# A list scheduler's view of its transfers: places in a queue instead of one rate, and a new table of shifts

## The chip, the core and the metric

The kernel runs on one core of one Trainium2 chip. A core has five engines with a queue of instructions each: PE (matrix products), ACT (activation functions), DVE (vector work), POOL (a second, slower vector engine) and SP, which here only issues transfers (DMAs). The engines run side by side and wait for each other by semaphores. The metric is the device time of one execution in microseconds (us); three runs of the kernel before gave 899.85, 899.12 and 898.61, so the median is 899.12 us.

## The reference

One transformer block on x, 2048 tokens of 1024 numbers in bfloat16. The attention is computed in four segments of 512 tokens, with 32 heads of width 32, and carries a memory M from segment to segment:

```python
x1 = layernorm(x)
q, k, v = (split_heads(x1 @ w) for w in (wq, wk, wv))       # each 1024 x 1024
for s in range(4):                                          # segments of 512 tokens
    a_dot = softmax(q[s] @ k[s].T * scale + mask) @ v[s]
    a_mem = (phi(q[s]) @ M) / (phi(q[s]) @ z + 1e-6)        # phi(t): t + 1 if t > 0, else exp(t)
    o[s] = g * a_mem + (1 - g) * a_dot                      # g = sigmoid(beta), one per head
    M += phi(k[s]).T @ v[s];  z += phi(k[s]).sum(rows)
h = x + o @ wo
h2 = h + (silu(layernorm(h) @ w1) * (layernorm(h) @ w3)) @ w2   # w1, w3: 1024 x 3584, w2: 3584 x 1024
```

## The kernel before, in words

The program does not write its instructions in the order in which they run. Each method of the class `Kernel` records operations in a graph (`Graph.op`, L282), with the buffers that they read and write, an estimated cost for each engine that could do them, and a class (a small number goes first). At the end `Graph.schedule` (L341) runs through a model of the five engines in time: whenever an engine is free in the model, it takes the ready operation with the lowest class and, within a class, the lowest number. The order so found on each engine is then emitted (`Graph.emit`, L523), with semaphore waits where an operation depends on another engine or on a transfer. So the costs in the model never reach the chip; the order that they lead to does. In the chip each engine, SP too, follows its order strictly.

Operations are gathered in units, counted up by `stage()`. The table `SHIFT` at the top gives for a unit a number that is added to its operations' numbers and one of -1, 0, 1 that is added to their class. The table is a result of a search and carries no other meaning.

The work, in the order in which `run` records it:

- **q, k, v** (`qkv`, `project`): for each segment and each half of the heads, three weights of 1 MB (1024 x 512) are loaded into one of three buffers `wp` (two later on), and four blocks of 128 x 512 per weight are made by eight matmuls each. In the trace these are L760 with `wp` beside `xnT` or `hnT`, the normalised and transposed x. ACT or DVE copies each block out of PSUM (L783, L784). A `wp` buffer can be loaded anew only when the last matmul that reads it is done.
- **normalisation** (`ln1`): x is loaded into one of four buffers `xs`, normalised by DVE (statistics L887, L890, scaling L902) and transposed by a transfer (`dma_t`, L332) into `xnT`, or into buffers named `hnT` that are free at that time.
- **attention** (`attention`, `scores`, `finish`): for each segment and half, ten groups of score matmuls (L1096) that use PE in four row strips, each followed by an exponential on ACT (L1110, 128 x 2048 numbers) and a mask on POOL (L1119); then column-strip matmuls for sums and products with v (L1197) and for the memory (L1178). The keys' phi is transposed by a transfer too (`pkn<-pk`).
- **normalising factors** (L1243 and on): for segments 2 and 3 the reciprocals are written to DRAM (`r_scr<-T`) and read back with every row repeated over 32 partitions: eight transfers of 256 KB for each half (L1288), four into `R0w` and four into `R`. The retrieval from the memory (L1323, PE in 16 tiles) waits for the four in `R`.
- **output projection** (`wo_stage`): eight matmuls per 128 x 512 block with `wo` and `oT`, x added (L1369), the sum h stored in `h_scr`, normalised and transposed into `hnT`.
- **up and down projection** (`ffn_up`, `ffn_down`): weights `w1b`, `w3b` of 512 KB in two buffers each, seven `w2b` of 1 MB, loaded once; matmuls L760 with `hnT` or `hm`. They fill PE between the pieces of attention of the last two segments, and alone from about 390 us on.

How the old scheduler sees a transfer: SP is busy for 400 ns (a transposition 1250 ns) for the issue; then all transfers are served one after the other at 260 bytes per ns, with the bytes of some kinds scaled by a factor; and the data are there 1560 ns after the service ends:

```python
begin = max(o.end, dma_free)
dma_free = begin + o.bytes / self.DMA_RATE
done = dma_free + self.DMA_FIX
```

All transfers are issued by SP, from `dma` (L325), `dma_t` (L332) or `copies` (L1288). The functions that the diff touches:

## Time and profile before

| | before |
|---|---|
| median of three runs | 899.12 us |
| the profiled execution, its own time | 899.22 us |
| its span, first to last instruction | 897.5 us |
| PE busy | 872.9 us (97%), 5733 recorded matmuls |
| DVE, ACT, POOL busy | 440.6, 303.5, 186.5 us |
| granted PE clock | 1.0 of full speed |
| moved by DMA | 105.75 MB |

The profile is of one execution. "Busy" is time in which the engine works on at least one instruction; matmuls overlap, so their durations do not add up to it. The view of waits puts each idle stretch of an engine down to what ended it: another engine's instruction, a transfer (named by what it writes and reads), or "issue", when nothing that the profile shows was waited for. In SP's timeline an entry is the issue of a transfer, not the transfer itself; from issue to landing is told apart. Some matmuls, 88 of 5821, have no record.

### The profile page before, as it was taken

The numbers are of one execution on the slowest core, as the hardware profiler recorded it, in microseconds if no ns is written. First come the engines' busy times: TensorE is split into PE (matmuls) and PEld (weight loads), VectorE is DVE, ScalarE is ACT, GpSimd is POOL, SyncE is SP. The second block draws the span as 40 slices with busy tenths as digits, with TensorE's granted clock in tenths as the row PEclk, the third lists the DMA queues.
The fourth block names the chain that finished last, engine by engine and source line by source line (L and its number), as shares of the span: only waits on it lengthen the run. The fifth ranks groups of instructions, "written<-read, shape, count | busy, mean of one in ns | idle before, by whom it ended". The sixth has DMA issues, their size and how long they took to land.

```text
span 897.5 us, 13708 instructions
## 1 busy us (share of the span) xinstructions
PE 872.9 (97%) x5733; PEld 398.7 (44%) x5821; DVE 440.6 (49%) x690; ACT 303.5 (34%) x347; POOL 186.5 (21%) x233
## 2 busy tenths in 40 slices
PE   8989899999999999999999999999999999999998
PEld 5343444444434344444444444444444444444445
DVE  5777768777566676747562132113333343323111
ACT  6857685767746464611110010001111111101000
POOL 2544344644352542612100000000000000000000
PEclk9999999999999999999999999999999999999999
DMA  7699867364791728368943014112212232200310
GB/s 238 161 236 228 194 179 175 118 147 125 195 198 56 166 70 165 94 223 228 271 127 95 20 49 116 47 47 76 65 53 74 67 95 61 80 18 1 94 36 24
DMA packets 148796, 105.75 MB, mean 118 GB/s; under 512 B 46336, under 2 KB 134400, under 8 KB 147712
## 3 DMA queue, kind: packets, MB, share of 16 engines
q1 hardware_dynamic: 148736, 104.89, 44.6%
q8 instruction: 46, 0.75, 0.4%
q14 instruction: 14, 0.11, 0.0%
HBM read 84.94 MB, written 9.44 MB: 105 GB/s over the span
## 4 chain that ended last, share of the span: by engine, by line
PE 88%; DMA 7%; DVE 1%; issue 1%; SPq 1%; ACT 1%; POOL 0%; DVEq 0%; ACTq 0%
PE ps L760 82%; PE ps L1197 3%; DMA R<-r_scr 3%; PE ps L1096 2%; DMA wp<-in_A_wq_dram 1%; DMA wp<-in_A_wv_dram 1%; SPq L1288 1%; DMA wp<-in_A_wk_dram 1%; DMA hnT<-xs 1%; DMA r_scr<-T 1%; ACT et L1110 0%; SPq L332 0%; PE ps L1178 0%; DVE oT L1303 0%; PE ps L1323 0%
## 5 line engine op out<-in xcount | busy, mean ns | idle before, releaser
L760 PE MATMUL ps<-hnT,w1b 128*128 128x512 bf16 x876 | 225.1, 379 | 2.0 <-issue 1.3
L760 PE MATMUL ps<-hnT,w3b 128*128 128x512 bf16 x878 | 225.3, 379 | 1.1 <-issue 0.2
L1399 ACT ACTIVATE sg<-ps 128x512 bf16<-128x512 f32 x112 | 66.9, 597 | 413.0 <-PE ps L760 407.9
L760 PE MATMUL ps<-w2b,hm 128*128 128x512 bf16 (+2 forms) x930 | 197.6, 366 | 1.2
L1402 DVE SCALAR_TENSOR_TENSOR t<-sg,ps 128x512 bf16<-128x512 bf16 x112 | 76.8, 686 | 180.1 <-ACT sg L1399 179.8
L1110 ACT ACTIVATE et<-ps 128x2048 bf16<-128x2048 f32 x80 | 150.0, 1875 | 42.6 <-PE ps L1096 42.3
L760 PEld LDWEIGHTS ps<-w2b,hm 128*128 128x128 bf16 x952 | 90.9, 98 | 102.9
L760 PEld LDWEIGHTS ps<-hnT,w3b 128*128 128x128 bf16 x896 | 86.7, 98 | 105.5 <-issue 2.6
L760 PEld LDWEIGHTS ps<-hnT,w1b 128*128 128x128 bf16 x896 | 86.0, 98 | 105.5 <-issue 3.8
L1119 POOL TENSOR_SCALAR_AFFINE_SELECT et<-et 128x512 bf16<-128x512 bf16 x96 | 92.8, 973 | 130.7 <-ACT et L1110 129.2
L1407 DVE SCALAR_TENSOR_TENSOR hm<-t,ps 128x512 bf16<-128x512 bf16 x112 | 76.2, 686 | 62.3 <-PE ps L760 60.9
L1432 DVE TENSOR_TENSOR ob<-hr,ps 128x512 bf16<-128x512 bf16 (+2 forms) x34 | 22.3, 656 | 109.0 <-PE ps L760 108.5
L760 PE MATMUL ps<-hnT,wp 128*128 128x512 bf16 x249 | 60.1, 380 | 4.9 <-DMA wp<-in_A_wk_dram 2.0
L760 PE MATMUL ps<-xnT,wp 128*128 128x512 bf16 (+1 forms) x343 | 60.4, 320 | 3.8 <-DMA wp<-in_A_wk_dram 1.4
L760 PE MATMUL ps<-wo,oT 128*128 128x512 bf16 x252 | 60.0, 379 | 0.2
L1133 DVE TENSOR_TENSOR sum<-sum,et 128x512 bf16<-128x512 bf16 (+1 forms) x64 | 42.8, 673 | 10.4 <-POOL et L1119 5.9
L760 PEld LDWEIGHTS ps<-xnT,wp 128*128 128x128 bf16 x352 | 27.7, 98 | 29.8 <-issue 3.2
L760 PEld LDWEIGHTS ps<-hnT,wp 128*128 128x128 bf16 x256 | 23.1, 98 | 34.1 <-issue 4.1
L760 PEld LDWEIGHTS ps<-wo,oT 128*128 128x128 bf16 x256 | 24.2, 98 | 30.2 <-issue 2.1
L760 PE MATMUL ps<-wp,xnT 128*128 128x512 bf16 x124 | 30.6, 380 | 2.2 <-DMA wp<-in_A_wv_dram 1.8
L1339 POOL TENSOR_TENSOR oT<-Nsb,R 128x512 bf16<-128x512 f32 x22 | 30.0, 1381 | 8.3 <-DVE lnmv L890 5.7
L1096 PE MATMUL ps<-qT,kT 32*128 32x128 bf16 (+3 forms) x512 | 31.7, 301 | 0.0
(97 smaller groups left out, 563.9 us busy)
## 6 DMA issues: line engine op xcount, KB each, us to landing
w1b<-in_B_w_dram SPq DMA_DIRECT2D x28, 512.0 KB, 3.9
w3b<-in_B_w_dram SPq DMA_DIRECT2D x28, 512.0 KB, 4.2
wp<-in_A_wv_dram SPq DMA_DIRECT2D x8, 1024.0 KB, 6.4
wp<-in_A_wk_dram SPq DMA_DIRECT2D x7, 1024.0 KB, 6.5
wp<-in_A_wq_dram SPq DMA_DIRECT2D x7, 1024.0 KB, 5.7
w2b<-in_B_w_dram SPq DMA_DIRECT2D x7, 1024.0 KB, 8.2
xs<-in_A_x_dram SPq DMA_DIRECT2D x16, 256.0 KB, 5.8
h<-in_A_x_dram SPq DMA_DIRECT2D x16, 256.0 KB, 3.4
```

The lines of the kernel that those rows point to most:

```text
L760: return [e.matmul(p[0](gr), p[1], p[2], start=p[3], stop=p[4]) for p in part]
L1096: ins.append(e.matmul(self.bank(gr, j, 512 - 128 * kc, off), k[r, g0 + g, 128 * kc:128 * kc + 128], q[r, g0 + g, 128 * kc:512], start=True ...
L1110: return [e.activation(et[:, :, :], src, AF.Exp, scale=self.scale)]
L1119: self.pool_op(lambda e, v=v, pat=pat: e.affine_select(v, v, pattern=pat, compare_op=ALU.is_ge, fill=0.0, base=0, channel_multiplier=-1), ...
L1133: lambda e, gr: [e.tensor_tensor(out, x, y, op=ALU.add)], reads=[x, y],
L1197: ins.append(e.matmul(self.ps[32 * i:32 * i + 32, b * 512 + c0:b * 512 + c0 + n], lhsT(i, kc, j), rhs(i, j), start=kc == 0 and j == first, ...
L1288: o.emit = lambda e, gr, to=to, src=src: [e.dma_start(to, src)]
L1339: self.either(lambda e, out=out, Ns=Ns, R1=R1: e.tensor_tensor(out, Ns, R1, op=ALU.add), 512, 2, [Ns, R1], [out], 2)
L1399: self.g.op("act", act_ns(512), lambda e, gr, sg=sg: [e.activation(sg, self.bank(gr), AF.Tanh, scale=0.5)], writes=[sg], cls=0, group=gg)
L1402: e.scalar_tensor_tensor(t1, sg, 1.0, self.bank(gr), op0=ALU.add, op1=ALU.mult)], reads=[sg], writes=[t1], cls=0,
L1407: e.scalar_tensor_tensor(dst, t1, 0.5, self.bank(gr), op0=ALU.mult, op1=ALU.mult)], reads=[t1], writes=[dst], cls=0,
L1432: self.g.op("dve", dve_ns(n), lambda e, gr, hs=hs, ob=ob, n=n: [e.tensor_tensor(ob, hs, self.bank(gr, 0, n), op=ALU.add)], reads=[hs], wri ...
```

## The change

Two things change, both in the scheduler's model.

First, a transfer is described by five numbers of its kind in place of its bytes: the time of its issue on SP, the places that it needs in a queue to be issued, the places that it holds while it is served, its time of service, and the time from the end of service to landing. The queue has 128 places. The new method `room` looks at the transfers still being served, lets each give back its places evenly over its service, and says when enough are free; the issue begins then, and SP stands until it ends. The table `LOADS` holds the numbers for twelve kinds; a transposition (`turn`) needs 92 places, a weight (`w`) 20. The nine first loads have a time of service of their own in place of a scale. `copies` and `dma_t` go through the same function `load`.

Second, the table `SHIFT` is another one: 577 entries instead of 570; of the 556 units that both have, five keep their pair. It was chosen by a search over the new model, with copies of the model that were disturbed.

The computation, the buffers, the sizes of the transfers and the numbers of matmuls (5821) and transfers (272) stay the same; the order on every engine is another one, and three operations that either DVE or POOL may do fall to DVE.

```diff
--- before.py
+++ after.py
@@ -28,103 +28,104 @@
 SHIFT = {
-    0: (-224, 0), 3: (7, 1), 4: (125, 0), 5: (120, 0), 6: (30, 0), 7: (0, 1), 8: (-28, 1),
...
-    596: (-75, 0), 597: (246, 0), 598: (3396, -1), 599: (0, 1), 600: (-6, 1),
+    0: (0, -1), 3: (952, 1), 4: (-2010, 1), 5: (170, -1), 6: (3510, 0), 7: (3489, -1),
...
+    597: (0, 1), 598: (224, 1), 599: (-1370, -1), 600: (2374, 1),
 }
...
@@ -193,8 +194,18 @@
     PAGE = 1024
     LAT = {"pe": 260.0, "act": 110.0, "dve": 110.0, "pool": 130.0, "dma": 150.0}
     SWITCH = 105.0
-    DMA_RATE = 260.0
-    DMA_FIX = 1560.0
+    PLACES = 128
+    LOADS = {
+        "x": (438, 56, 6, 717, 1449), "w": (382, 20, 42, 3722, 1419),
+        "first": (436, 30, 68, 1765, 1450), "beta": (339, 20, 12, 86, 2063),
+        "turn": (1240, 92, 38, 923, 1415), "wo": (314, 70, 0, 1236, 1437),
+        "store": (339, 50, 8, 679, 1397), "up": (370, 50, 50, 1872, 1611),
+        "rows": (422, 2, 6, 1208, 1631), "down": (385, 58, 28, 3150, 1386),
+        "hr": (433, 2, 32, 818, 1538), "out": (333, 0, 12, 367, 1011),
+    }
+    KINDS = (("xs", "x"), ("h_scr", "store"), ("r_scr", "store"), ("hr", "hr"), ("hn", "x"),
+             ("h", "x"), ("wp", "w"), ("wo", "wo"), ("w1b", "up"), ("w3b", "up"),
+             ("w2b", "down"), ("beta", "beta"), ("out", "out"))
     BEGIN = 800.0
 
     def __init__(self, nc, es):
@@ -316,22 +327,37 @@
         self.ops.append(o)
         return o
 
-    def dma(self, out, in_, cls=5, deps=(), scale=1.0):
-        n = 1
-        for s in out.shape:
-            n *= s
-        o = self.op("sp", 400.0, None, reads=(in_,), writes=(out,), cls=cls, deps=deps,
+    def load(self, out, in_, emit, kind, cls, deps=(), serve=None):
+        issue, need, held, time, land = self.LOADS[kind]
+        o = self.op("sp", issue, emit, reads=(in_,), writes=(out,), cls=cls, deps=deps,
                     kind="dma")
-        o.emit = lambda e, g: [e.dma_start(out, in_)]
-        o.bytes = n * SIZE[out.dtype] * scale
+        o.load = need, held, serve or time, land
         return o
 
+    def dma(self, out, in_, cls=5, deps=(), serve=None, kind=None):
+        name = out.tensor.name
+        kind = kind or next(k for n, k in self.KINDS if name.startswith(n))
+        return self.load(out, in_, lambda e, g: [e.dma_start(out, in_)], kind, cls, deps, serve)
+
     def dma_t(self, out, in_, cls=5):
 
-        o = self.op("sp", 1250.0, None, reads=(in_,), writes=(out,), cls=cls, kind="dma")
-        o.emit = lambda e, g: [e.dma_start_transpose(out, in_)]
-        o.bytes = 130000
-        return o
+        return self.load(out, in_, lambda e, g: [e.dma_start_transpose(out, in_)], "turn", cls)
+
+    @staticmethod
+    def room(line, now, need):
+
+        line[:] = [x for x in line if x[1] > now]
+        left = [(max(b, now), e, held * (e - max(b, now)) / (e - b)) for b, e, held in line]
+        over = sum(x[2] for x in left) + need - Graph.PLACES
+        t = now
+        for b, e, held in left:
+            if over <= 0:
+                break
+            if held > 0:
+                part = min(over, held)
+                t = b + part / held * (e - b)
+                over -= part
+        return t
 
     def stage(self):
 
@@ -354,6 +380,7 @@
         order = {e: [] for e in ENGINES}
         mode = None
         dma_free = 0.0
+        line = []
         n_done = 0
         seqno = 0
         waiting = []
@@ -452,6 +479,8 @@
                         begin = max(begin, held["dve"])
                     elif e == "dve" and o.port:
                         begin = max(begin, until["pool"])
+                    if o.kind == "dma":
+                        begin = self.room(line, now, o.load[0])
                     o.end = begin + cost
                     until[e] = o.end
                     if e == "dve" and o.port:
@@ -465,8 +494,9 @@
                     done = o.end + lat
                     if o.kind == "dma":
                         begin = max(o.end, dma_free)
-                        dma_free = begin + o.bytes / self.DMA_RATE
-                        done = dma_free + self.DMA_FIX
+                        dma_free = begin + o.load[2]
+                        done = dma_free + o.load[3]
+                        line.append((begin, dma_free, o.load[1]))
                     seqno += 1
                     heapq.heappush(events, (done, seqno, "done", o))
                     if o.users and e == "pe":
@@ -931,7 +961,7 @@
         for i in range(4):
             t = 4 * s + i
             x = self.xs[i][:, :]
-            self.g.dma(x, self.x2d[t * 128:(t + 1) * 128, :], cls=2, scale=0.65)
+            self.g.dma(x, self.x2d[t * 128:(t + 1) * 128, :], cls=2)
             self.ln(t, x, x, 4 + s)
             self.g.dma_t(self.xnT[s][:, :, i * 128:(i + 1) * 128], x, 3)
 
@@ -968,7 +998,7 @@
                 continue
             for kind in "qkv":
                 w, src = self.weights(kind, half)
-                self.g.dma(w[:, :, :], src, cls=1, scale=0.87)
+                self.g.dma(w[:, :, :], src, cls=1)
                 for i in range(4):
                     self.project(s, kind, half, i, w)
 
@@ -978,13 +1008,13 @@
         (wq, sq), (wk, sk), (wv, sv) = (self.weights(kind, 0) for kind in "qkv")
         dma = self.g.dma
         x = [(self.xs[t][:, :], self.x2d[t * 128:(t + 1) * 128, :]) for t in range(4)]
-        loads = [x[0] + (0.66,), x[1] + (0.66,), x[2] + (1.2,),
-                 (wq[:, :, 0:256], sq[:, :, 0:256], 1.19), x[3] + (0.7,),
-                 (wk[:, :, 0:256], sk[:, :, 0:256], 0.89),
-                 (wq[:, :, 256:512], sq[:, :, 256:512], 0.89),
-                 (wk[:, :, 256:512], sk[:, :, 256:512], 0.89), (wv[:, :, :], sv, 1.11)]
-        for out, in_, scale in loads:
-            dma(out, in_, cls=0, scale=scale)
+        loads = [x[0] + (780,), x[1] + (670,), x[2] + (1230,),
+                 (wq[:, :, 0:256], sq[:, :, 0:256], 2400), x[3] + (720,),
+                 (wk[:, :, 0:256], sk[:, :, 0:256], 1790),
+                 (wq[:, :, 256:512], sq[:, :, 256:512], 1790),
+                 (wk[:, :, 256:512], sk[:, :, 256:512], 1790), (wv[:, :, :], sv, 4520)]
+        for out, in_, serve in loads:
+            dma(out, in_, cls=0, serve=serve, kind="x" if serve < 1500 else "first")
         self.applied = []
         for t in range(4):
             self.first_tile(t)
@@ -1271,7 +1301,7 @@
             rm = Rc[:, 1, :, :].rearrange("p j b -> p b j") if not both else Rc[:, :, :, :].rearrange("p t j b -> p b t j")
             G.op("pool", 300.0 + 100 * both, lambda e, gr: [e.tensor_copy(td, rm)], reads=[rm], writes=[td], cls=2)
             self.dve_op(lambda e: e.transpose(T2, T1), dve_ns(512), [T1], [T2], 2)
-            G.dma(rd, T2, cls=2, scale=0.5)
+            G.dma(rd, T2, cls=2)
 
         rd = self.rd[128 * (2 * (s % 2) + half):128 * (2 * (s % 2) + half) + 128, :]
 
@@ -1282,11 +1312,9 @@
             for i in range(4):
                 to = tile[32 * i:32 * i + 32, :, :].rearrange("p j n -> p (j n)")
                 of = rd[32 * i + row:32 * i + row + 4, :]
-                o = G.op("sp", 420.0, None, reads=(of,), writes=(to,), cls=2, kind="dma")
-                o.bytes = 312000
                 src = bass.AP(of.tensor, of.offset, [[0, 32], [1, 2048]])
-                o.emit = lambda e, gr, to=to, src=src: [e.dma_start(to, src)]
-                ops.append(o)
+                ops.append(G.load(to, of, lambda e, gr, to=to, src=src: [e.dma_start(to, src)],
+                                  "rows", 2))
             return ops
 
         rows0 = rows and s in ROWS0
@@ -1356,7 +1384,7 @@
             t = 4 * s + i
             h, hn = self.h[t % 2], self.hn[0]
             self.g.stage()
-            self.g.dma(h[:, :], self.x2d[t * 128:(t + 1) * 128, :], cls=2, scale=0.72,
+            self.g.dma(h[:, :], self.x2d[t * 128:(t + 1) * 128, :], cls=2,
                        deps=(self.mark,) if t < 2 else ())
             for half in range(2):
                 self.g.stage()
@@ -1369,7 +1397,7 @@
                 self.g.op("dve", dve_ns(512), lambda e, gr, hs=hs: [e.tensor_tensor(
                     hs, hs, self.bank(gr), op=ALU.add)], reads=[hs], writes=[hs], cls=1,
                     group=gr)
-            self.g.dma(self.hd[t * 128:(t + 1) * 128, :], h[:, :], cls=3, scale=0.5)
+            self.g.dma(self.hd[t * 128:(t + 1) * 128, :], h[:, :], cls=3)
             self.ln(16 + t, h[:, :], hn[:, :], 6)
             self.g.dma_t(self.hnT[s][:, :, i * 128:(i + 1) * 128], hn[:, :], 2)
 
@@ -1412,7 +1440,7 @@
         if blk == 0:
             for i in range(7):
                 self.g.dma(self.w2[i][:, :, :], self.B_w2[i * 512:(i + 1) * 512, :].rearrange(
-                    "(j p) n -> p j n", p=128), cls=5, scale=0.87)
+                    "(j p) n -> p j n", p=128), cls=5)
         for i in range(8):
             t = 8 * blk + i
             hr = self.hr[t % 3]
```

## The prediction

> **What bounds the kernel now.** I read the page first: its own span line, the busy shares and the chain that ended last.
>
> ```profile
> span 897.5 us, 13708 instructions
> PE 872.9 (97%) x5733; PEld 398.7 (44%) x5821; DVE 440.6 (49%) x690; ACT 303.5 (34%) x347; POOL 186.5 (21%) x233
> PE 88%; DMA 7%; DVE 1%; issue 1%; SPq 1%; ACT 1%; POOL 0%; DVEq 0%; ACTq 0%
> ```
>
> PE is the bound: 897.5 - 872.9 leaves 24.6 us in which it does nothing. Busy PE time cannot be shortened by an order: the clock is 1.0 throughout, and both programs hold the same 5821 matmuls with the same 189 changes between full-array, row-tiled and column-tiled groups (counted in the two orders). So only those 24.6 us are in play. Windows of 50 us tell where they lie (start and end, length, then busy us and count of PE, weight loads, DVE, ACT and POOL, the clock, DMA share and GB/s); this one stands for the nine from 400 us on:
>
> ```profile
> 500.00:550.00 50.00, 49.74 (x229) 22.67 (x232) 12.97 (x19) 4.78 (x8) 0.00 (x0) 1.00 0.19 53
> ```
>
> Its 0.26 us missing are lost records (229 of 232). Behind 400 us nothing is to be had but the last 2.4 us, where the final output leaves. Before 20 us the start waits for x and the first weights (some 3.5 us); both orders issue the same first nine loads. That leaves 20 to 320 us. There the view of waits, for PE alone, says who ended the idle time (us in total, times, longest):
>
> ```profile
> PE ps L760 <- DMA wp<-in_A_wk_dram: 3.4, 2, 2.0
> PE ps L760 <- issue: 2.9, 18, 0.2
> PE ps L760 <- DMA wp<-in_A_wv_dram: 2.7, 3, 1.0
> PE ps L760 <- DMA hnT<-xs: 1.5, 1, 1.5
> PE ps L1197 <- issue: 1.4, 1, 1.4
> PE ps L1323 <- DMA R<-r_scr: 1.2, 2, 0.9
> PE ps L760 <- DMA wp<-in_A_wq_dram: 0.3, 1, 0.3
> ```
>
> Transfers: 3.4 + 2.7 + 1.5 + 1.2 + 0.3 = 9.1 us in nine waits. The 2.9 us of "issue" are sixteen-odd pieces of 0.2 us behind a change of tiling; they stay. The largest wait, in SP's timeline and PE's (start, us, instruction):
>
> ```profile
> 94.46 0.40 SPq L325 DMA_DIRECT2D wp<-in_A_wv_dram  x1
> 95.54 1.92 SPq L332 DMA_TRANSPOSE xnT<-xs  x1
> ...
> 99.38 2.69 SPq L332 DMA_TRANSPOSE hnT<-xs  x1
> 102.17 2.48 SPq L332 DMA_TRANSPOSE pkn<-pk  x1
> 104.70 0.58 SPq L325 DMA_DIRECT2D wp<-in_A_wk_dram  x1
> ```
> ```profile
> 108.25 1.03 PE L760 MATMUL ps<-wo,oT 128*128 128x512 bf16 x4
> 111.27 1.04 PE L760 MATMUL ps<-hnT,wp 128*128 128x512 bf16 x4 [1.99 <-DMA wp<-in_A_wk_dram]
> ```
>
> An issue of L332 takes 1.24 us when little is in flight, and 1.9 to 2.7 here, behind 1 MB of wv. SP issues in order, so the load of wk starts at 104.70 and lands at 111.2, and PE stands for 2 us. Three such places (wk at 111 and 249 us, wv at 241) cost 2.0 + 1.4 + 1.0 = 4.4 us of the 9.1. The old scheduler gave an issue a fixed 1250 or 400 ns and never saw this.
>
> [...] between 94 and 113 us the landings follow the issues, 0.6 to 1.3 us apart for 256 KB. [...] here the up-projection puts 50 into 10.79 us (49 recorded), 215.8 ns.
>
> **The change, part by part.** The capacity of 128 places, the table of costs and `room` exist only in the scheduler; they emit no instruction and no wait. What reaches the chip is another order, chosen through another table of shifts. Counts: PE 5821 and SP 272 in both, DVE 690 to 693, ACT 331 in both, POOL 235 to 232 (three operations that may run on either). Three DVE operations at 0.7 us add 2 us to an engine that is 49% busy; cover: its own idle time; without cover at most 2 us. Cost taken: 0.
>
> The value lies in the distances. For each load I count the PE work from the last matmul that reads the old buffer to the first that needs the new one: 215.8 ns per 512-column matmul, 0.42 us per group of scores (0.65 for some with 256 columns), 0.46 us for the retrieval's sixteen tiled matmuls, 4 to 5 us for a whole column block. Against it stands the need: 5.4 us from issue to landing when alone (median 6.6 over all, with company 6.8), 0.1 us of semaphore and about 0.3 us until the last matmul is through: 5.85 us alone, some 6.9 in company.
>
> ```profile
> DMA to landing us min/median/max: 5.1/6.6/9.3
> ```
>
> Place by place, what before waits for and what the new order does there:
> - wk at 111 (2.0) and wv at 101 (0.9): the crowd on SP is still there (h, wo, three transposes), but wv is no longer ahead of it. Without the 3.7 us of service of 1 MB ahead, the transposes are through before the release. The wq behind them has 24 matmuls, two scores of 0.42 and one of 0.65: 6.67 us. Wk follows with 32 matmuls and four scores: 8.7. I leave 0.5 us at wq.
> - wv at 241 (1.0) and wk at 249 (1.4): now 40 matmuls and four scores (10.1 us) and 24 matmuls with a column block (9.5): both gone.
> - wv at 51 (0.8), wq at 36 (0.3): these two kinds recur: loads with 24 matmuls and two or three scores, 6.0 us against 5.85. Of such places the new order has five (wk three times, wq, wv), most with nothing beside them. I leave 0.2 us each for one with wo behind it and for one of 24 matmuls and the retrieval, 5.18 + 0.46 = 5.64.
> - hnT at 63 (1.5): the transpose is now issued some 33 us of PE work ahead instead of 9: gone.
> - R at 259 and 310 (0.3 and 0.9): distance 24.4 and 15.3 us instead of 16.5 and 14.4. The second also no longer waits for the eighth R row in line: R1 and R0w alternate and PE needs the seventh, 1.2 us less. I leave 0.3.
>
> Left over: 0.5 + 0.4 + 0.3 = 1.2 us. For what distances cannot show (a transposition or store whose DVE input comes late, with weights behind it on SP) I add as much again, 1.3 us: bounds 0 and, if every one of some ten tight loads takes 0.5 us, 5 us. The "issue" wait of 1.4 us in the middle of a column group I don't understand and leave as it is. A stall taken away moves the whole rest forward, since PE is then never idle. Sum: 9.1 - 1.2 - 1.3 = 6.6 us. Profiled execution: 897.5 us of span and 1.7 around it are 899.2; minus 6.6 gives 892.6; the median of 899.12 stands 0.1 under it: **892.5 us**.
>
> What is late next: PE would wait on PSUM evacuations by DVE and ACT. I compared the shortest chain (matmul, evacuation, next matmul in that bank) with the PE work between, for the 298 and 296 such waits up to 400 us: under 0.5 us to spare are 5 before and 9 after, nearly all in the first 10 us, where 0.2 to 0.4 us may be added.
>
> **Rivals.**
> - *Half is given back.* The loads stay tight by design (6.0 against 5.85 us), and one landing of 0.5 to 1 us more in company comes back at six or seven places: 4 us on top of 2.5. Gain 9.1 - 6.5 = 2.6: 896.5 us. For it: wv at 44 us, with a transpose right behind, took 6.8 us instead of 5.4.
> - *Nothing moves.* The transfers were only the last to arrive, and something else (ACT's exponentials, 1875 ns each, or the POOL mask) is ready just behind: 899 +- 1.8. Against it: where PE waited for a transfer the others had been done; for it: DVE is 68 to 80% busy in every 50 us up to 250 us.
> - *Slower, by late evacuations.* The new classes put normalisation (DVE L887, L902) or sums (L1133) in front of evacuations. Each time PE waits one DVE operation, 0.65 us. It turns the sign above 6.6 us, that is from ten such hits, and shows as slower from thirteen; with twenty: 892.5 + 13 = 905.5 us. For it: nearly 300 waits of this kind; against it: before shows one only (0.6 us at 71 us), with much the same spare times.
> - *The change does not do what it says*, the order being nearly the old one: excluded, since PE, DVE and SP orders differ in most places up to 460 us.
>
> **How the numbers follow.** Forecast (887.5 to 895): 0.66. Half given back (895 to 897.3): 0.16. Nothing moves (897.3 to 900.9, 0.2%, about what a measurement of this kernel can tell from no change): 0.08. Slower: 0.10. Faster is 0.66 + 0.16 = 0.82. Range: the low end if all 9.1 go and the odd 1.4 with them: 888.5; the high end takes in the half and some of no change: 898.0.
>
> **What would show it.** Right: in 20 to 320 us PE's waits on wk, wv, hnT and R sum to 1 to 4 us; at the wq load that follows h, wo and three transposes near 100 us SP issues within 0.5 us of the release; PE busy stays 872 to 874 us. Wrong: new waits on wp above 1 us each, PE waits on DVE or ACT above 2 us in sum, or SP lines where a transpose waits for DVE with a weight load behind it.

## The result, and the profile after

| | before | after |
|---|---|---|
| median of 12 runs | 899.49 us (897.39 to 905.36) | 902.23 us (897.20 to 905.05) |
| ratio after / before | | 1.0023, 95% interval 1.0000 to 1.0046 |
| the profiled execution, its own time | 899.22 us | 905.05 us |
| its span | 897.5 us | 903.3 us |
| mean granted PE clock in it | 1.0 | 0.992 |

The forecast was 892.5 us, 888.5 to 898.0. The changed kernel is not faster; it is slower by about what can be told from no change. A second set, 22 runs beside 33 of before, gave 1.0018 (1.0002 to 1.0034). The time falls outside the range, on the wrong side.

The page of the kernel after, the same three lines that were shown of before (span; busy shares; the chain that ended last):

```profile
span 903.3 us, 13791 instructions
PE 886.5 (98%) x5821; PEld 400.6 (44%) x5821; DVE 447.8 (50%) x693; ACT 303.9 (34%) x347; POOL 183.3 (20%) x230
PE 92%; DMA 5%; DVE 1%; issue 1%; SPq 1%; ACT 0%; POOL 0%
```

PE is busy for 13.6 us more, with the same matmuls. A part of that is bookkeeping: this trace holds all 5821 records of matmuls, that of before 5733. The sixteen-odd "issue" pieces of 0.2 us that the prediction took for a stall behind a change of tiling are missing here, so they were lost records and no stall. The rest is the clock, below.

PE's waits in the after kernel between 20 and 320 us (us in total, times, longest):

```profile
PE ps L790 <- DMA wp<-in_A_wq_dram: 4.6, 2, 2.4
PE ps L790 <- DMA h<-in_A_x_dram: 3.0, 1, 3.0
PE ps L790 <- DMA wp<-in_A_wk_dram: 1.7, 1, 1.7
PE ps L1351 <- issue: 1.1, 1, 1.1
PE ps L1126 <- ACT et L1140: 0.7, 1, 0.7
...
PE ps L790 <- DMA wp<-in_A_wv_dram: 0.3, 1, 0.3
```

L790 here is L760 of before, L1351 is L1323. The "issue" of L1351 ends 0.09 us behind the landing of the last R row, so it is a wait for R. Transfers: 4.6 + 3.0 + 1.7 + 1.1 + 0.3 = 10.7 us in six waits, where before had 9.1 in nine. The waits have become fewer and longer; the longest was 2.0 us and is now 3.0. Wv, hnT and wk at 111 us, which the forecast struck out, are indeed gone; others came.

The clock is the second thing. Short windows of the kernel after (start and end, length, then busy us and count of PE, weight loads, DVE, ACT, POOL, the granted clock, DMA share, GB/s):

```profile
67.50:70.90 3.40, 1.17 (x9) 0.31 (x7) 0.00 (x0) 2.74 (x4) 1.50 (x3) 1.00 1.03 284
71.00:74.30 3.30, 3.30 (x9) 1.17 (x8) 2.74 (x6) 0.50 (x1) 0.83 (x3) 0.50 1.07 280
74.50:77.90 3.40, 3.40 (x24) 1.39 (x22) 1.40 (x3) 2.37 (x2) 0.63 (x2) 1.00 0.34 102
```

PE waits for wq until 70.71. From 70.91 to 74.32 us, for 3413 ns, the clock is 0.50, and PE gets 9 matmuls done in 3.3 us where the window behind it does 24, smaller ones among them. The clock records of this execution hold three such stretches: 3413 ns from 70.91, 3413 ns from 115.29, 6827 ns from 152.83, each at the end of one of the three longest waits. Such a stretch of 3413 ns at half speed is called a half window below. Together they are 13.65 us at half speed, which is 6.8 us of work lost. Before's record has none between its 4th microsecond and its end.

The profiled pair, 903.3 - 897.5 = 5.8 us, is then: clock +6.8; waits for transfers +1.6; PE's waits in the first 20 us -1.7 (3.7 before, 2.0 after); the "issue" waits in the column groups (L1197 and L1178 of before, L1227 and L1208 of after) -1.2 (1.9 before, 0.7 after). Sum 5.5. The last term is not the order's doing: in a second profile of after, used below, these waits are 1.7 us again.

### The profile page after: what moved, and what is told of

It reads as the page before. It is cut to its first block, busy times and chain, and to the rows that moved or that the text cites. A ratio compares the mean times of both kernels' runs of the same rounds, so it can differ in the third digit from the quotient of the medians.

```text
span 903.3 us, 13791 instructions
## 1 busy us (share of the span) xinstructions
PE 886.5 (98%) x5821; PEld 400.6 (44%) x5821; DVE 447.8 (50%) x693; ACT 303.9 (34%) x347; POOL 183.3 (20%) x230
## 4 chain that ended last, share of the span: by engine, by line
PE 92%; DMA 5%; DVE 1%; issue 1%; SPq 1%; ACT 0%; POOL 0%
PE ps L790 87%; PE ps L1126 3%; DMA wp<-in_A_wq_dram 2%; PE ps L1227 2%; DMA wp<-in_A_wk_dram 1%; DMA hnT<-xs 1%; DMA h<-in_A_x_dram 0%; ACT et L1140 0%; DMA beta<-in_A_beta_dram 0%; SPq L340 0%; SPq L344 0%; PE ps L1351 0%; DVE sum L1163 0%; PE ps L1208 0%; POOL et L1149 0%
## 5 line engine op out<-in xcount | busy, mean ns | idle before, releaser
L790 PE MATMUL ps<-hnT,w1b 128*128 128x512 bf16 x896 | 227.7, 379 | 0.0
L790 PE MATMUL ps<-hnT,w3b 128*128 128x512 bf16 x896 | 227.3, 379 | 0.0
L790 PE MATMUL ps<-w2b,hm 128*128 128x512 bf16 (+2 forms) x952 | 198.4, 366 | 0.0
L790 PEld LDWEIGHTS ps<-w2b,hm 128*128 128x128 bf16 x952 | 90.8, 98 | 103.2 <-DMA hr<-h_scr 0.4
L790 PEld LDWEIGHTS ps<-hnT,w3b 128*128 128x128 bf16 x896 | 86.9, 98 | 105.5 <-issue 2.1
L790 PEld LDWEIGHTS ps<-hnT,w1b 128*128 128x128 bf16 x896 | 86.1, 98 | 105.3 <-issue 4.6
L790 PE MATMUL ps<-wo,oT 128*128 128x512 bf16 x256 | 65.2, 391 | 3.1 <-DMA h<-in_A_x_dram 3.0
L790 PE MATMUL ps<-hnT,wp 128*128 128x512 bf16 x256 | 63.6, 394 | 4.6 <-DMA wp<-in_A_wq_dram 4.6
L790 PE MATMUL ps<-xnT,wp 128*128 128x512 bf16 (+1 forms) x352 | 60.9, 321 | 2.5 <-DMA wp<-in_A_wk_dram 1.7
L1163 DVE TENSOR_TENSOR sum<-sum,et 128x512 bf16<-128x512 bf16 (+1 forms) x64 | 45.0, 702 | 10.8 <-POOL et L1149 6.4
L790 PEld LDWEIGHTS ps<-xnT,wp 128*128 128x128 bf16 x352 | 27.9, 98 | 28.9 <-issue 2.7
L790 PEld LDWEIGHTS ps<-hnT,wp 128*128 128x128 bf16 x256 | 24.2, 101 | 36.9 <-issue 9.9
L790 PEld LDWEIGHTS ps<-wo,oT 128*128 128x128 bf16 x256 | 24.2, 99 | 34.8 <-issue 4.8
L790 PE MATMUL ps<-wp,hnT 128*128 128x512 bf16 x128 | 31.5, 381 | 0.3 <-DMA wp<-in_A_wv_dram 0.3
```

What stands on the lines that cost most here:

```text
L790: return [e.matmul(p[0](gr), p[1], p[2], start=p[3], stop=p[4]) for p in part]
L1163: lambda e, gr: [e.tensor_tensor(out, x, y, op=ALU.add)], reads=[x, y],
```

## The experiments

All edits but two (the empty tables at the end) stand in `run`, directly behind the scheduler, and act on the finished order. The helpers are these; an index i is the i-th transfer of SP's queue as the scheduler left it. The comments in these diffs are added here.

```diff
         self.g.schedule()
+        G = self.g
+        sp, pe = G.order["sp"], G.order["pe"]
+        loads = list(sp)
+        def behind(i, j):            # transfer i goes directly behind transfer j on SP
+            sp.remove(loads[i])
+            sp.insert(sp.index(loads[j]) + 1, loads[i])
+        def fill(i, n):              # n matmuls ident x ident ahead of the first PE operation that waits for load i
+            t = next(o for o in pe if loads[i] in o.deps)
...
+            f.deps = {d: r for d, r in t.deps.items() if d.kind != "dma"}
+            pe.insert(pe.index(t), f)
```

The results in one table. "To before" is the mean minus the mean of the runs of before in the same set (27 to 59 of them; mean clock 0.9986 to 0.9990). There are four sets, on different chips, and the means of before in them lie between 898.7 and 899.7 us; so kernels of different sets are compared by this column and not by their means. "Without clock" takes 0.9 us for each 0.001 by which the mean clock lies below that of before, or adds it where it lies above; 0.9 is a thousandth of the time. The ratios' intervals are +-0.0011 to +-0.0027, that is 1.0 to 2.4 us to either side.

| kernel | runs | mean us | mean clock | to before | without clock |
|---|---|---|---|---|---|
| after, second set | 22 | 901.3 | 0.9965 | +1.6 | -0.3 |
| after, waits filled | 12 | 902.5 | 0.9995 | +2.8 | +3.5 |
| after, waits half filled | 22 | 896.3 | 1.0000 | -3.0 | -1.7 |
| before, waits half filled | 22 | 898.9 | 0.9995 | -0.6 | 0.0 |
| after, h first | 22 | 898.1 | 0.9975 | -1.4 | -2.5 |
| after, wq and wk first | 22 | 900.2 | 0.9959 | +0.7 | -1.9 |
| after, pkn later | 22 | 900.8 | 0.9960 | +2.1 | -0.6 |
| after, h_scr later | 22 | 899.6 | 0.9966 | +0.9 | -1.2 |
| after, R0w rows later | 11 | 902.0 | 0.9945 | +3.3 | -0.7 |
| after, these five together | 6 | 891.9 | 0.9987 | -7.8 | -7.8 |
| after, with xs1 too | 6 | 890.0 | 0.9997 | -9.3 | -8.4 |
| before, first set of moves | 6 | 904.3 | 0.9967 | +4.8 | +2.9 |
| before, second set of moves | 15 | 902.7 | 0.9973 | +4.1 | +2.6 |

**The changed kernel again.**

> The changed kernel again, beside the kernels that vary it. Both theories: about 902 us. The clock theory (PE waits above some 2 us cost half-speed windows of 3.4 us, worth 1.7 us each) expects runs between 897 and 905 us whose time follows the mean granted clock at about 1.7 us per 0.002; the theory that the order alone is slow expects the scatter not to follow the clock.

Mean 901.3 us, 897.5 to 909.9 (two runs above the 905 that was expected). Pooled with the first set, 34 runs: clock 1.0, 3 runs, mean 898.7; 0.998, 12 runs, 900.1; 0.996, 12 runs, 901.7; 0.994, 5 runs, 904.2; below, 2 runs, 905.0 and 909.9. Before, pooled over four sets, 176 runs: clock 1.0, 86 runs, 898.0; 0.998, 77 runs, 899.9; 0.996, 10 runs, 902.6; 0.994, 3 runs, 905.6. In both kernels the time follows the clock by 0.7 to 1.3 us per 0.001, around the pure loss of 0.9; at the same clock the two kernels differ by 0.9 us at most down to 0.996. The mean clocks, 0.9965 and 0.9988, mean (1 - clock) x 900 / 1.7 = 1.9 half windows in a run of after and 0.6 in one of before. That is 2.1 us of the 2.3 us by which the pooled means (901.6 and 899.2) differ.

**How long a stall must be.** Ten stalls of graded length in the last feed-forward part of the kernel before, where nothing else disturbs:

```diff
+        for k, n in enumerate((3, 5, 7, 9, 11, 13, 9, 7, 11, 15)):
+            stand(len(pe) - 380 + 34 * k, n)   # PE waits for a chain of n POOL memsets that starts when its last operation is done
```

> The kernel before with ten stalls of PE put into the last up-projection and down-projection, 34 PE units apart, each held by a chain of 3, 5, 7, 9, 11, 13, 9, 7, 11 and 15 small POOL operations (some 1 to 4 us). Nothing else is changed. Clock theory: the short stalls leave the clock at 1.0, those above about 2 us are followed by one or two windows of 3.4 us at 0.5, and the time grows by the stalls (some 25 us) plus 1.7 us for each window. Rival, the windows come from the load of PE in the attention part and not from idle time: no half-speed window here.

One run: 935.0 us, clock 0.989. The stalls came out as 0.85, 1.37, 1.89, 2.42, 2.94, 3.55, 2.42, 1.89, 3.03 and 3.98 us (the view of waits gives the sum, the times and the longest):

```profile
PE ps L760 <- POOL ones L1475: 24.3, 10, 4.0
```

The clock records of this run hold six half windows, 10.2 us of lost work. With the 24.3 us that is 34.5; the run took 36.4 us more than before's runs with clock 1.0 in the same set (mean 898.6, from 897.3 to 901.7). Windows of this run, on the grid that its clock records show (one edge every 3413 ns, counted from the first edge on record at 4.48 us), a stall and the window behind it, three times:

```profile
704.30:707.50 3.20, 0.59 (x2) 0.31 (x4) 0.00 (x0) 0.00 (x0) 2.04 (x10) 1.00 0.11 32
707.70:711.00 3.30, 3.30 (x9) 1.14 (x8) 1.09 (x2) 0.60 (x1) 0.00 (x0) 0.50 0.00 0
772.50:775.80 3.30, 0.88 (x5) 0.28 (x4) 0.09 (x1) 0.00 (x0) 1.84 (x9) 1.00 0.00 0
776.00:779.20 3.20, 3.20 (x9) 1.21 (x8) 0.80 (x2) 0.60 (x1) 0.00 (x0) 0.50 0.02 5
806.70:810.00 3.30, 1.60 (x8) 0.78 (x9) 0.46 (x1) 0.00 (x0) 1.29 (x7) 1.00 0.14 40
810.10:813.40 3.30, 3.30 (x17) 1.50 (x16) 0.81 (x2) 0.60 (x1) 0.00 (x0) 1.00 0.00 0
```

Idle for 2.7 or 2.4 us of a window: the next one runs at 0.50. Idle for 1.8 us: it runs at 1.00. What counts is idle time within one window of the grid: the other stall of 2.42 us, at 672.02 to 674.44 us, lies across an edge (1.47 + 0.95) and costs nothing. So the load of the attention part isn't needed for it; the rival falls. Over the traces of after and of all runs here but the two with an empty table and the half-filled after, which has no clock records, behind the first edge on record and with pieces of idle time above 0.2 us summed, each of the 21 windows with 2.09 us or more of idle time is followed by a half one. Of those with up to 1.94 us, one is (1.86 us, right behind one of 1.94), apart from three that were at half speed themselves. That is one reason why the times of one kernel scatter: its waits lie differently on the grid in each run. (It is not the only one: the 86 runs of before with clock 1.0 still lie between 895.8 and 901.7 us, and what else varies stays open.) The second profile of after is such a case. It has a wait for h of 3.4 us and the clock stays at 1.00, the wait being cut in 1.9 and 1.4 (fields as above):

```profile
146.20:149.60 3.40, 1.47 (x7) 0.49 (x5) 2.99 (x4) 1.71 (x1) 2.18 (x2) 1.00 1.43 182
149.65:153.00 3.35, 1.81 (x15) 0.74 (x17) 0.00 (x0) 0.55 (x1) 0.00 (x0) 1.00 0.19 43
```

**Filling the waits.** The idle matmuls keep PE busy (at wq near 70 us 36 of them took 2.18 us and 18 took 1.18, so each further one 56 ns) and move no transfer:

```diff
+        for i, n in ((32, 36), (55, 36), (66, 48), (91, 26)):   # wq 70 us, wq 114, h 153, wk 248
+            fill(i, n)
```

> The changed order with its four longest transfer waits (wq at 70 and 114 us, h at 153, wk at 248) filled by idle matmuls of PE that go to the bank about to be started: 36, 36, 48 and 26 of 56 ns, or 2.0, 2.0, 2.7 and 1.5 us. No transfer is moved, so the stall is as long. Clock theory: the half-speed windows behind these waits vanish, clock 1.0 in all runs, 897 to 899.5 us, some 3 us less than the changed kernel (its mean clock of 0.9965 times 902 us). Rival, the clock falls for another reason, or the falls cost nothing: 902 us or above, since nothing else is shortened.

The clock rose to 0.9995, but the mean is 902.5 us: a miss of 3 to 5.5 us. With half of them (18, 18, 24, 13):

> As the run with filled waits, with half the idle matmuls at the same four places: 18, 18, 24 and 13 of 56 ns (1.0, 1.0, 1.3, 0.7 us), so that they end before the transfer lands also where it lands early, and leave 1.0 to 1.7 us idle. Theory that idle time of more than 2.0 us within one 3.4-us window halves the clock in the next (largest without: 1.94 us, smallest with: 2.23 us): clock 1.0 in nearly all runs. If such windows are what makes the changed kernel slower than before, the mean is 898 to 899.5 us, 2 to 3 us below the changed kernel. Rival, the half windows cost no time (the full filling took them away and won nothing): 901 to 902.5 us.

The clock is given as 1.0 for all 22 runs. The profiled one holds no clock records, but its matmuls bear the figure out: several 512-column matmuls in a row that start some 430 ns apart in place of 216, which every half window on record here shows, stand only in its first 6 us. The mean is 896.3 us, ratio 0.9967 (0.9953 to 0.9981): the same order of transfers, 73 small matmuls more, and 4.6 us less than the changed kernel, each against its own before (-3.0 and +1.6), where 2 to 3 had been expected. The clock explains 3.2 of them, and the intervals take in the other 1.4. PE's waits of this run, all of the span:

```profile
PE ps L790 <- DMA wp<-in_A_wk_dram: 3.0, 2, 2.2
PE ps L790 <- DMA wp<-in_A_wq_dram: 1.9, 2, 1.1
...
PE ps L790 <- DMA h<-in_A_x_dram: 0.5, 1, 0.5
```

Most of the waiting is still there (5.6 us with 0.2 for wv, beside 4.1 us of filling: 9.7 us, where the two profiles of after have 10.7 and 12.2). So it is not waiting alone that made the changed kernel slower than before. Why the full filling cost 5.7 us more than the half one, each against its own before, is not settled: it has 73 matmuls more, 4.1 us, which would be on the path wherever a load lands early; 1.6 us remain.

The same for the kernel before, at its six longest waits (6, 12, 6, 16, 8, 10):

> The kernel before, treated as the changed one was: 58 idle matmuls of 56 ns at its six longest transfer waits (6, 12, 6, 16, 8 and 10, that is 0.3 to 0.9 us each, about half of each wait). Clock theory: before has a mean clock of 0.9986, so half windows take 0.0014 x 899 = 1.3 us of it; with the fillings the clock is 1.0 and the mean 898 us. The order alone, without the clock, is then worth 898 - 896.3 = 1.7 us, and the clock made a loss of it. Rival, the fillings help for another reason (they gave the changed kernel 5 us where its clock explains 3.2): 895 to 896.5 us here too, and the two orders are worth the same.

898.9 us, -0.6 to its own before, where -1.3 was expected for the clock; the clock rose by 0.0007 and not to 1.0, which is just these 0.6 us. 895 to 896.5, if fillings helped for another reason, is out. With both orders filled, the new one leads by 3.0 - 0.6 = 2.4 us. So the order by itself is worth something between nothing (0.3 us, from the second set without the clock) and 2.4 us.

**Moving the transfers in front.** What makes the waits? In the traces of before and after all 272 issues of SP run in the program's order, each beginning behind the end of the one ahead of it, and the landings on record (272 and 262) come in the same order. SP's queue in the second profile of after, near the wait for h (start, us of issue, instruction), and PE at that wait:

```profile
138.75 1.24 SPq L344 DMA_TRANSPOSE xnT<-xs  x1
140.03 5.88 SPq L344 DMA_TRANSPOSE pkn<-pk  x2
146.43 0.36 SPq L340 DMA_DIRECT2D h<-in_A_x_dram  x1
```
```profile
151.03 1.04 PE L790 MATMUL ps<-wo,oT 128*128 128x512 bf16 x4 [3.36 <-DMA h<-in_A_x_dram]
```

Two transposes that can wait hold SP for 5.88 us, with 1.25 MB in flight (wv and a store of h); in quiet one takes 1.24. DVE has read the old h by 143.43 us (its `hn` is written then), so the load could have started there; it starts behind the transposes, 3.0 us later. Five such places were changed:

```diff
+        for i in (52, 53, 54):                     # w1b, xs2, xs3 behind wq and wk, near 105 us
+            behind(i, 56 if i == 52 else i - 1)
+        behind(64, 66)                             # two transposes of pkn behind h, near 143 us
+        behind(65, 64)
+        behind(29, 35)                             # a transpose of pkn behind wq and wk, near 56 us
+        behind(90, 91)                             # a store of h_scr behind wk, near 239 us
+        for i in (120, 122, 124, 126):             # four R0w rows behind the last R row, near 308 us
+            behind(i, 125 if i == 120 else i - 2)
```

> The changed order with eleven transfers moved a few places later on SP: w1b, xs2 and xs3 behind wq and wk near 105 us; the two transposes of pkn near 143 us behind the load of h; one of pkn near 56 us behind wk; the store of h_scr near 239 us behind wk; four R0w rows near 308 us behind the last R1 row. Theory that SP's crowd makes the waits: the five waits of 2.4, 2.2, 3.0, 1.7 and 1.1 us sink below 1 us each, no half-speed window is left, 888 to 892 us. Rival, the waits come from the rate of the transfers and not from their order on SP: 899 to 903 us, the waits turn up at the moved transfers' readers or at the next weights.

891.8 us median, ratio 0.9917 (0.9897 to 0.9937), in the range of the first theory. Half windows are not all gone, as it had said they would be: three of the six runs have a clock of 0.996 or 0.998. In the profile, two of the waits for transfers in 20 to 320 us are left:

```profile
PE ps L790 <- DMA wp<-in_A_wq_dram: 1.7, 1, 1.7
...
PE ps L790 <- DMA wp<-in_A_wk_dram: 0.5, 1, 0.5
```

The second profile of after had 12.2 us of them (wq 4.6, h 3.7, wk 1.9, wv 1.0, R 1.0); ten went with eleven transfers moved in SP's order. The remaining wq was still held by a load of xs1 that itself waited for a transpose; moved too, with 8 idle matmuls in the rest of the wait:

```diff
+        behind(31, 32)
+        for i, n in ((32, 8),):
+            fill(i, n)
```

> The kernel with moved transfers, and in it also xs1 moved behind wq near 63 us (its wait for a transpose held wq up), with 8 idle matmuls (0.45 us) in what remains of that wait. SP theory: wq is issued 1 to 2 us earlier, its 1.7 us of waiting go to some 0.5, no half window behind it, 889.5 to 891 us. Rival, wq is slow because of its company: 891.5 to 892.5 us, as without.

889.9 us median, ratio 0.9896 (0.9870 to 0.9923), the lowest mean of this study; the wait is 0.8 us, the mean clock 0.9997. That is as the first theory said, but 1.5 us against the kernel with the five groups, each to its own before, is less than six runs can tell apart.

Then each group of moves alone, on the changed kernel.

> The changed kernel with one move only: the two transposes of pkn near 143 us go behind the load of h that PE waits for at 153 us (wait of 3.0 to 3.4 us, twice a half window behind it in the profile of the first run). SP theory: h is issued about 4 to 6 us earlier, the wait goes, and with it part of the half windows: 3 to 4.5 us less than the changed kernel, 897 to 898 us, mean clock up by 0.001. Rival, another wait takes its place within a few us (the wq behind, or a transpose of pkn that comes late): 900 to 901.5 us.

898.1 us, 3.0 less than after (each to its own before), as the first theory said. SP now:

```profile
143.91 0.34 SPq L340 DMA_DIRECT2D h<-in_A_x_dram  x1
144.29 2.91 SPq L344 DMA_TRANSPOSE pkn<-pk  x2
```

DVE reads the old h until 143.82, the load is issued at once, and PE's wait for it is gone. The transposes behind it take 2.9 us for two, with 256 KB of other transfers in front of them in place of 1.25 MB.

> The changed kernel with one move only: w1b, xs2 and xs3 near 105 us go behind wq and wk. wq was issued 1.1 us behind its release and landed 8.0 us later, PE waited 2.2 us. SP theory: issued at once and with less in front, the wait goes: 2 to 3.5 us less than the changed kernel, 898 to 899.5 us. Rival, the three transfers were not in its way (the transposes ahead of them are): 900.5 to 902 us.

900.2 us, 1.0 less: between the two expectations. In its profile the wait at wq near 114 us is gone, and wk waits 2.8 us near 244 us.

> The changed kernel with one move: the transpose of pkn near 56 us, whose issue took 4.7 us, goes behind wq and wk. Theory of single places: wq is issued earlier or lands sooner, its wait of 2.3 us at 70 us shrinks to the 1.5 of the kernel with all moves: 0.8 us, with the half window behind it up to 1.5 us: 899.8 to 900.5 us. Theory that the moves work together: 901 to 902 us, and wq waits as long, for xs1 holds SP up too.

900.8 us: the wait for wq at 70 us is gone in the profile (one wq wait of 2.2 is left, near 110), but the R wait is 2.4 us instead of 1.0, and the sum hardly moves. Against its own before it is 0.5 us more than after, as for moves that work together.

> The changed kernel with one move: a store of h_scr near 239 us goes behind wk. Single places: wk's wait of 1.8 us at 244 to 248 us shrinks by 1 to 1.5 us: 899.5 to 900.5 us. Together: within 0.5 us of the changed kernel (901.3).

899.6 us. By the figure this is as for single places; but before ran 1.0 us faster in this set than in that of after, and against it the gain is 0.7 us, between the two. Wk waits 0.6 us instead of 1.8.

> The changed kernel with one group of moves: four R0w rows near 308 us go behind the last R1 row. R1's last row then lands some 3.5 us earlier, the wait of 1.0 to 1.1 us at 319 us goes. Single places: 900.2 us (1.1 less). Together, or if another operand of the retrieval is late: 901 to 902 us.

902.0 us, so the single place does not pay here. R waits 0.4 us instead of 1.0, but the mean clock is the lowest of all, 0.9945, that is about three half windows in a run; the profile shows two, both at h.

The five differences to the changed kernel (-3.0, -1.0, +0.5, -0.7, +1.7, each against its own set of before) add up to -2.5 us; together the moves give -9.5. Without the clock they are -2.2, -1.6, -0.3, -0.9 and -0.3, sum -5.3, against -7.5, and the intervals of five kernels cover the rest. A single mend leaves other waits for a load above 2 us and the half windows behind them; all together leave no wait above 1.7 us in the profile. Why the clock is lowest with the R0w rows moved is not known.

**Can the old order be mended in the same way?** Moves on the kernel before, first with two transposes behind wk near 100 us, xs1 behind a transpose near 56, h1, h_scr and a transpose behind wk near 240, a transpose behind wv near 235, R0w rows and w1b behind R:

```diff
+        for i, j in ((52, 54), (53, 52), (28, 29), (91, 92), (95, 98), (96, 95), (97, 96),
+                     (117, 125), (118, 117), (119, 118), (120, 119), (121, 120)):
+            behind(i, j)
```

> The kernel before with some of its own SP transfers moved as in the changed one: two transposes (hnT, pkn) near 100 us behind wk; xs1 near 56 us behind the transpose of xs0; a transpose near 235 us behind wv; a transpose, h and the store of h_scr near 240 us behind wk; w1b and four R0w rows near 297 us behind the last R1 row. Theory that such waits are made by what SP issues just ahead, in either order: PE waits for wk at 111 us (2.0), hnT at 63 (1.5), wv at 241 (1.0), wk at 249 (1.4), R at 310 (0.9) shrink by 4 to 6 us in sum: 893 to 896 us. Rival, only the new table's order can be mended so: 898 to 900 us.

904.3 us: wrong by 8 us and more. Wk near 101 us was issued 3 us earlier (101.65 instead of 104.70) and landed at the same time (111.35, before 111.22), 9.7 us after its issue instead of 6.5. The greater part of this lay in front of it: wv had not landed when it was issued, and the last transfer ahead of it landed 5.1 us after its issue (106.72), before 3.4 (108.11). From there wk took another 4.6 us, before 3.1; these 1.5 us may be the two transposes now right behind it. That this can happen is seen at wv near 44 us of before, which has nothing in flight in front and a transpose issued 0.43 us behind: 6.7 to 7.2 us in the five traces that have this place, where 42 of 49 loads of a weight with nothing beside them took 4.9 to 5.6. And PE waited 3.7 us for DVE's addition of h. I took the moved load of h for the cause and left it alone in a second set, together with the moves near 56 and 100 us:

```diff
+        for i, j in ((91, 92), (95, 98), (97, 95), (117, 125), (118, 117), (119, 118), (120, 119), (121, 120)):
+            behind(i, j)
```

> The kernel before with those of its moves that shortened a wait: a transpose near 235 us behind wv, a transpose and a store near 240 us behind wk, w1b and four R0w rows near 297 us behind the last R1 row. Theory that such waits belong to what SP issues just ahead, in either order: the waits for wv at 241 us (1.0), wk at 249 (1.4) and R at 310 (0.9) shrink by 2 to 3 us: 896.5 to 897.7 us. Rival, a mend at one place of the old order comes back as a wait at the next: 898.7 us or above.

902.7 us, and the wait of 3.7 us is still there. So the load of h was not it. DVE and PE in that run:

```profile
242.81 0.93 DVE L902 TENSOR_SCALAR hn<-h,lnst,rstd 128x1024 bf16<-128x1024 bf16 x1 [6.17 <-DMA hnT<-hn]
243.66 1.27 DVE L1369 TENSOR_TENSOR h<-h,ps 128x512 bf16<-128x512 bf16 x2
```
```profile
245.07 2.62 PE L760 MATMUL ps<-wp,xnT 128*128 128x512 bf16 x8 [3.75 <-DVE h L1369]
```

The transpose that both sets put behind wv reads `hn`, of which there is one buffer. Until it has landed DVE cannot write the next `hn`; DVE stands for 6.17 us, the addition of h behind it is late, and PE waits for its PSUM bank. Here transposes of `pkn` could be put off and this one of `hn` could not, though both look alike in SP's queue. The rival of this run, that the mend comes back as a wait at the next place, held. The set without this transpose was not run, so whether the old order can be mended like the new one stays open.

**Which part of the change.** Both schedulers with an empty table:

```diff
-SHIFT = {
...
+SHIFT = {}
```

> The changed scheduler with an empty table of stage shifts: the queue of transfers alone. Theory that the gain of the queue is real and the table only polishes it: 905 to 915 us, at least 5 us faster than the old scheduler with an empty table. Rival, the time is made by the table (a choice among many tries), the model adds little: 910 to 930 us, within 5 us of the old scheduler or above it.

> The old scheduler with an empty table of stage shifts. First theory: 912 to 925 us, 5 or more above the queue alone. Rival: 910 to 930 us, within 5 us of the queue alone or below it.

933.6 us for the queue and 929.9 for the old rate, two runs each. The first theory (the queue 5 us or more ahead) falls. With 0.9 us for each 0.001 of clock (0.9800 and 0.9835) taken off they are 915.6 and 915.1 us: the model's queue of 128 places by itself gives no better order than the rate; either time is made by its table. Each table under the other scheduler was not run.

## Why the prediction was wrong

Two steps of the prediction failed: that the clock is a constant, and the need of a load that it set against the distances.

*"Busy PE time cannot be shortened by an order: the clock is 1.0 throughout."* This step failed. The matmuls are the same, but the clock at which they run depends on where the order lets PE wait. A mean of 1.9 half windows per run against 0.6, worth 2.1 us, is nearly the whole difference of 2.3 us between the two kernels' means; the half-filled waits bear it out, which brought the clock of the new order to 1.0 and its time down by 4.6 us. The forecast read the clock of one execution of before as a property of the program; with 90 of 176 runs of before below 1.0 it isn't. The sign "PE busy stays 872 to 874" came out at 886.5 in the first profile and at 873.6 in the second, whose clock is 1.0. In the trace of before the longest wait was 2.0 us, just below the 2.09 that cost.

*"Left over: 1.2 us", and 1.3 for what distances cannot show.* This term of the sum failed by more: 2.5 us was said, it is 10.7 us in the first profile and 12.2 in the second. Place by place in the first:

| place in after | said | measured | what was late |
|---|---|---|---|
| wq at 114 us | 0.5 | 2.4 | issued 1.0 us behind its release, since xs3 waited for a transpose; landed 8.0 us later |
| wq at 70 | 0.2 at most | 2.2 | issued 1.6 late behind xs1, landed 7.8 later |
| h at 153 | in the 1.3 | 3.0 | issued 3.0 late, behind 5.9 us of issue of two pkn transposes |
| wk at 248 | gone | 1.7 | issued 2.4 late, landed 8.5 us behind its issue, a transpose, h and a store in front |
| R at 319 | 0.3 | 1.1 | last of seven rows in line, 8.7 us to landing |
| wv, hnT, wk at 111 | gone | 0.3 | as said |

The distances were right; the need set against them was not. 5.85 us is what a weight takes alone, and 6.9 was allowed in company; these took 7.8 to 8.5, and SP itself issued them 1.0 to 2.4 us late, h 3.0. The table of issues says the same at the median (tensor, KB, median us to landing); for before wq had 5.7 and h 3.4:

```profile
wp<-in_A_wq_dram SPq DMA_DIRECT2D x7, 1024.0 KB, 7.3
...
h<-in_A_x_dram SPq DMA_DIRECT2D x16, 256.0 KB, 4.4
```

The sign "SP issues within 0.5 us of the release" came out at 1.0 (the last matmul on the old buffer is done at 105.4 us). SP's queue there (start, us of issue):

```profile
99.42 4.38 SPq L344 DMA_TRANSPOSE hnT<-xs  x2
103.90 0.53 SPq L340 DMA_DIRECT2D w1b<-in_B_w_dram  x1
105.15 1.19 SPq L340 DMA_DIRECT2D xs<-in_A_x_dram  x2
106.38 0.43 SPq L340 DMA_DIRECT2D wp<-in_A_wq_dram  x1
```

The step looked only at whether the transposes were through (its 3.7 us of service for 1 MB are an estimate; the 284 GB/s of the window of after from 67.50 us give the same). They were, but three loads behind them, two of them waiting for one of these transposes to land (105.13 and 105.99 us), were not counted. The sign that PE's waits on wk, wv, hnT and R sum to 1 to 4 us came true with 1.7 + 0.3 + 0 + 1.1 = 3.1 us, and says little: it named what before had waited for, and 7.6 of the 10.7 us are for wq and h. The sign of being wrong, new waits on wp above 1 us each, came true three times.

*"What is late next" and the rival of late evacuations.* Right to give it little: PE's waits on ACT, DVE and POOL between 20 and 320 us are 0.7 + 0.2 us. That the kernel came out slower came true by another mechanism.

*The stall at the start and the "issue" wait of 1.4 us*, which I left as they were, went down by 1.7 and 1.2 us. The second term stands again in the second profile and is no gain of the order. With the clock set aside: 892.5 + (10.7 - 2.5) - 1.7 = 899.0 us, against 898.7 measured in the three runs with clock 1.0. This is the range of the rival "nothing moves", but not its mechanism (something else that is ready just behind the transfers): waits went at their old places and came at others. With 1.9 half windows of 1.7 us it is 902.2; the means of the two sets are 902.0 and 901.3.

*"Half is given back"* had the right mechanism, tight loads that land late in company. It gave 6.5 us of waits left, and all 9 and more were.

## What to carry to other kernels

A wait on PE is not worth its length alone: in these runs one that fills 2.1 us or more of a 3.4-us clock window costs another 1.7 us, so of two orders with the same sum of waits take the one with more and shorter waits, and where a wait can't be removed, half-fill it with matmuls that nobody reads. Half-filling paid in the new order (4.6 us) and gave 0.6 in the old, which is within the noise; filling a wait whole lost time. Price a tight load by what is issued just ahead of it, for SP stood still on two transposes for 5.9 us, and by a transpose just behind it, with which a weight took 6.7 to 7.2 us to landing in place of 4.9 to 5.6. Before a transfer is put off, ask which buffer it releases and for which engine: two transposes that read `pk`, of which there are two buffers, moved for a gain of 3 us; one that reads the single `hn` cost PE a wait of 3.7.

## What the runs showed of the hardware that I had not expected

- The granted clock halves for 3413 ns or a multiple of it (6827 in several runs, up to 13653 in the one with the queue and an empty table), on a grid of 3413 ns that doesn't move within a run: edges of the run with stalls at 707.62, 741.76, 775.89, 840.74 and 874.88 us, multiples of 3413 ns apart. 2.09 us of idle time or more in a window brought it in all 21 cases, 1.94 never by itself.
- The issue of a transpose took 1.24 us in quiet; two in a row took 2.9 us with 256 KB of other transfers in front, and 5.9 us behind 1.25 MB (a single one near 56 us: 4.7). SP issued nothing else meanwhile.
- A transpose issued 0.43 us behind a weight of 1 MB went with 6.7 to 7.2 us to landing, in five traces, where most such loads with nothing beside them took 4.9 to 5.6 us.
